# Output transposes in 64-row halves, and a plain product for the last 128 slots of the last expert

## The chip, the core and the metric

The kernel runs on one core of a Trainium2 chip. The core has five engines with instruction streams of their own: TensorE (PE; its weight loads are listed as PEld), VectorE (DVE), ScalarE (ACT), GpSimd (POOL) and SyncE (SP), and DMA queues that SP, ACT and POOL fill. They wait for each other through semaphores. The metric is the device time in microseconds (us) of one execution; lower is better. The profile is of one execution on its own.

## The reference

The first half is attention with a threshold, for 8 batches of 8 heads with 576 rows of 64: scores below the row's maximum less `tau` are dropped. Its output, as rows of 512, goes through one of eight experts, chosen by a hash of the token:

```python
scores = scale * np.matmul(q, k.transpose(0, 1, 3, 2))
thresh = np.max(scores, axis=-1, keepdims=True) - tau
scores = np.where(scores >= thresh, scores, -1000000000.0)
attn = np.exp(scores - np.max(scores, axis=-1, keepdims=True))
attn = attn / (np.sum(attn, axis=-1, keepdims=True) + 1e-09)
x = np.matmul(attn, v)                            # then (B,H,S,D) -> (B*S, H*D)
expert_idx = token_ids * np.int64(2654435761) % np.int64(E)
for e in range(E):                                # E = 8, N = 4608, D = 512, F = 1024
    mask = expert_idx == e
    h = np.maximum(x[mask] @ w1[e], 0.0)
    out[mask] = h @ w2[e]
```

## The kernel before

**Stages.** Attention runs over 32 pairs of heads and writes x to a scratch in DRAM. Beside it the tokens are sorted into slots: each expert has `CAP` = 608 slots, in five tiles (`kt` 0 to 4) of 128, 128, 128, 128 and 96. `stok` holds the token of every slot, and `gidx` the same as a table with a column per expert and tile, which the output scatters use (lines 744 to 750). From about 504 us on the experts run, one after the other. What doesn't fit into 608 slots is left to an overflow loop at line 989, which runs `n_ov` times, a number read from SBUF; with these inputs its body is skipped.

**An expert.** Activations lie transposed, features on partitions, slots along the free axis. Layer 1 is x times w1 with a Relu, layer 2 is h times w2. Both are done by `seven` (line 825), a Strassen-like scheme: each operand is cut into 2 by 2 blocks, seven block products take the place of eight, and sums of blocks are made on DVE. The slots are halved into `CH` = 304 columns, so a product streams 304 columns. A product of layer 2 is 8 matmuls in the source, each of which is two instructions on TensorE: 16 of 128 by 128 weights. `left` and `right` (lines 783 to 791) list the four sums of the weights and of the activations. They write one sum over one of the blocks itself (`a21` and `b12`), the other three into `w1_s`, `w2_s`, `x_s`, `h_s`. Each product lands in a PSUM tile of two banks (`bank2`, four of them in turn); ACT copies the first one to `p1`, and DVE adds the rest through `u2`, `u3`, `u4` into the outputs: h in layer 1, `oT` in layer 2.

**Output.** `oT` holds an expert's result transposed, 512 features as four blocks (`co`) of 128 partitions, by 608 slots. `put_out` (line 876) turns the named tiles back with TensorE transposes of 128 by 128 (line 882), copies each turned tile to an `o_sb` buffer (three in turn) and scatters its rows to `out` with an indirect DMA from POOL (line 894). Two tiles share one PSUM tile, one bank each.

**Order.** The order on each engine is the order in the source (`manual_schedule`), with side work hung between the seven products: `side1` and `side2` are called after each step. Expert e - 1's outputs go out in layer 1 of expert e, tiles (0, 1) after step 0, (2, 3) after step 1, (4) after step 2. The last expert has no successor: its tiles (0, 1) go out after step 4 of its layer 2, ahead of the seventh product, and (2, 3) and (4) when that is done (lines 977 and 978). SP loads the weights of later experts and moves turned x; POOL gathers x and scatters outputs.

**The same transposes elsewhere.** In the attention stage `turn` (line 266) and `early_xT` (line 554) turn 64 rows at a time: the two halves of the partitions, one after the other, into two different banks.

Of the kernel before, what the change touches and what calls it, by code (L numbers as in the profile page):

```python
# [9 lines left out]
FP32 = mybir.dt.float32  # L10
# [10 lines left out]
def kernel(  # L21
# [35 lines left out]
    KT, NB = 5, 19  # L57
    CAP = 32 * NB
# [69 lines left out]
    with tc.tile_pool(name="a_q", bufs=1) as a_q, \  # L128
# [496 lines left out]
        with tc.manual_schedule():  # L625
# [119 lines left out]
            for h in range(4):  # L745
                rows, n = slice(32 * h, 32 * h + 32), (NB - h + 3) // 4
                nc.vector.tensor_copy(gidx[rows, :, 0:n], stok[rows, :, h::4])
            for g in range(4):
                rows, n = slice(32 * g, 32 * g + 32), min(KT, NB - KT * g)
                nc.vector.tensor_copy(gidx_x[rows, 1:, 0:n], stok[rows, 1:, KT * g:KT * g + n])  # L750
# [8 lines left out]
    with tc.tile_pool(name="m_x", bufs=1) as m_x, \  # L759
# [4 lines left out]
        xT_bufs = [xT_0, m_x.tile([P, CO, CAP], FP32, name="xT_1")]  # L764
        xq = m_x.tile([P, DIN // 32, 32 * KT], FP32, name="xq")
        oT = m_x.tile([P, CO, CAP], FP32, name="oT")
        mark = m_x.tile([P, 1], FP32, name="mark")
        w1_s = m_s.tile([P, 3, C2, F2], FP32, name="w1_s")
        x_s = m_s.tile([P, 3, C2, CH], FP32, name="x_s")
        w2_s = m_s.tile([P, 3, FH, D2], FP32, name="w2_s")  # L770
        h_s = m_s.tile([P, 3, FH, CH], FP32, name="h_s")
        p1, u2, u3, u4 = (m_s.tile([P, 2, CH], FP32, name=n) for n in ("p1", "u2", "u3", "u4"))

        def bank2():
            return ps_m[0].tile([P, 2, 512], FP32, name="bank2")

        def sub(out, in0, in1):
            return lambda: nc.vector.tensor_tensor(out=out, in0=in0, in1=in1, op=ALU.subtract)

        def add(out, in0, in1):  # L780
            return lambda: nc.vector.tensor_tensor(out=out, in0=in0, in1=in1, op=ALU.add)  # L781

        def left(a11, a12, a21, a22, s):

            s2, s3, s4 = s
            return [sub(s3, a11, a21), add(a21, a21, a22), sub(s2, a21, a11), sub(s4, a12, s2)]

        def right(b11, b12, b21, b22, t):

            t2, t3, t4 = t  # L790
            return [sub(t3, b22, b12), sub(b12, b12, b11), sub(t2, b22, b12), sub(t4, b21, t2)]
# [4 lines left out]
        def w2_blocks(w):  # L796
            return [w[:, FH * j:FH * j + FH, D2 * i:D2 * i + D2] for i in range(2) for j in range(2)]
# [1 line left out]
        def x_blocks(x):  # L799
            return [x[:, C2 * j:C2 * j + C2, CH * k:CH * k + CH] for j in range(2) for k in range(2)]  # L800

        def h_blocks(c0, c1):
            return [h_0[:, FH * j + c0:FH * j + c1, CH * k:CH * k + CH]
                    for j in range(2) for k in range(2)]

        def triple(t, c0, c1):
            return [t[:, i, c0:c1] for i in range(3)]

        def sums_w1(e):
            return left(*w1_blocks(w_tiles[e, 1]), triple(w1_s, 0, C2))  # L810

        def sums_w2(e):
            return left(*w2_blocks(w_tiles[e, 2]), triple(w2_s, 0, FH))

        def sums_x(e):
            return right(*x_blocks(xT_bufs[e % 2]), triple(x_s, 0, C2))

        def sums_h(c0, c1):
            return right(*h_blocks(c0, c1), triple(h_s, c0, c1))

        def run(work, n=1):
            for _ in range(min(n, len(work))):
                work.pop(0)()

        def seven(a, a_s, b, b_s, m0, outs, relu, after):

            (a11, a12, s1, a22), (s2, s3, s4) = a, a_s
            (b11, t1, b21, b22), (t2, t3, t4) = b, b_s
            c11, c12, c21, c22 = outs
            n_k = a11.shape[1]  # L830

            def product(x, y):
                ps = bank2()
                for i in range(2):
                    c0 = m0 + P * i
                    for c in range(n_k):
                        nc.tensor.matmul(ps[:, i, 0:CH], lhsT=x[:, c, c0:c0 + P], rhs=y[:, c],  # L837
                                         start=c == 0, stop=c == n_k - 1)
                return ps[:, :, 0:CH]

            def out(c, ps, u, step):
                add(c, ps, u)()
                if relu:
                    nc.scalar.activation(c, c, AF.Relu)  # L844
                after(step)

            nc.scalar.copy(p1[:], product(a11, b11))  # L847
            out(c11, product(a12, b21), p1[:], 0)
            add(u2[:], product(s2, t2), p1[:])()
            after(1)  # L850
            add(u3[:], product(s3, t3), u2[:])()
            after(2)
            out(c21, product(a22, t4), u3[:], 3)
            k5 = product(s1, t1)
            add(u4[:], k5, u2[:])()
            out(c22, k5, u3[:], 4)
            out(c12, product(s4, b22), u4[:], 5)

        def layer1(e, side):

# [6 lines left out]

        def layer2(e, side):

            w = w_tiles.pop((e, 2))  # L870
            outs = [oT[:, C2 * i:C2 * i + C2, CH * k:CH * k + CH]
                    for i in range(2) for k in range(2)]
            seven(w2_blocks(w), triple(w2_s, 0, FH), h_blocks(0, FH), triple(h_s, 0, FH), 0, outs,
                  False, side)

        def put_out(e, kts):

            tr = bank2()
            for i, kt in enumerate(kts):
                rows = TROWS[kt]  # L880
                for co in range(CO):
                    nc.tensor.transpose(tr[0:rows, i, P * co:P * co + P],  # L882
                                        oT[:, co, FIRST[kt]:FIRST[kt] + rows], ident[:])
            for i, kt in enumerate(kts):
                rows = TROWS[kt]
                o_sb = m_o.tile([P, DIN], FP32, name="o_sb")
                if e == E - 1 and kt % 2:
                    nc.vector.tensor_copy(o_sb[0:rows], tr[0:rows, i])
                else:
                    nc.scalar.copy(o_sb[0:rows], tr[0:rows, i])  # L890
                put_rows(o_sb[0:rows], gidx[0:rows, e, kt:kt + 1])

        def put_rows(o_sb, idx):
            inst = nc.gpsimd.indirect_dma_start(  # L894
                out=out[:, :], out_offset=bass.IndirectOffsetOnAxis(ap=idx, axis=0),
                in_=o_sb, in_offset=None, bounds_check=N - 1, oob_is_err=False)
# [28 lines left out]
        with tc.tile_pool(name="ps_x", bufs=1, space=PSUM) as ps_x, tc.manual_schedule():  # L925
            run(sums_w2(0), 4)
            fill(18)
            late_h(lambda fo: (ps_sc.tile([P, 2, 512], FP32, name="sc") if fo in (2, 4) else
                               ps_x.tile([P, 2, 512], FP32, name="xT_ps")))
            fetch(1)  # L930
            run(sums_h(0, FH), 4)
        sc_stack.close()
        ps_m = [ctx.enter_context(tc.tile_pool(name="ps_m", bufs=4, space=PSUM))]

        with tc.manual_schedule():
            for e in range(E):
                more = e + 1 < E
                turns = turn_x(e + 1) if more else []

                if e > 0:  # L940
                    w2_work, h_work = sums_w2(e), sums_h(0, 2)
# [16 lines left out]
                    run(sums_h(2, FH), 4)  # L958
                if e + 2 < E:
                    load_w1(e + 2)  # L960
                x_work = (sums_w1(e + 1) + sums_x(e + 1)) if more else []

                def side2(step):
                    if step == 0:
                        run(turns, len(turns))
                        if e + 2 < E:
                            fetch(e + 2)
                    else:
                        run(x_work, 2)
                    if not more and step == 4:  # L970
                        put_out(e, (0, 1))

                layer2(e, side2)
                run(x_work, len(x_work))
                if e + 2 < E:
                    load_w2(e + 2)
            put_out(E - 1, (2, 3))
            put_out(E - 1, (4,))

        def relu_layer(w_sb, x_sb):  # L980
            for fo in range(FO):
# [71 lines left out]
```

## Time and profile before

| what | value |
| --- | --- |
| median of 3 runs | 956.54 us (956.51 to 958.95) |
| profiled execution, its own time | 963.93 us |
| its span, first to last instruction | 962.3 us |
| TensorE clock granted, mean | 0.997 |
| PE busy | 941.3 us, 98% |
| DVE, ACT, POOL busy | 738.2, 479.6, 302.4 us |
| all transposes of line 882 | 160 |
| all output scatters of line 894 | 40 |

An engine's busy time is read as a share of the span. PE at 98% means that its own work and what keeps it waiting set nearly all of the time. A row of the timeline names the start and length in us, the engine, the line, the operation, output<-input, the shape and how many instructions were merged. Matmuls overlap in the pipe, so that the length of one (0.419 us for 304 columns) is more than the distance to the next; the distances are what adds up. The rows of POOL's DMA_INDIRECT are the time to write the descriptors; the data moves afterwards.

### The profile page before, as it was taken

The numbers are of one execution on the slowest core, as the hardware profiler recorded it, in microseconds if no ns is written. First come the engines' busy times: TensorE is split into PE (matmuls) and PEld (weight loads), VectorE is DVE, ScalarE is ACT, GpSimd is POOL, SyncE is SP. The second block draws the span as 40 slices with busy tenths as digits, with TensorE's granted clock in tenths as the row PEclk, the third lists the DMA queues.
The fourth block names the chain that finished last, engine by engine and source line by source line (L and its number), as shares of the span: only waits on it lengthen the run. The fifth ranks groups of instructions, "written<-read, shape, count | busy, mean of one in ns | idle before, by whom it ended". The sixth has DMA issues, their size and how long they took to land.

```text
span 962.3 us, 20672 instructions
## 1 busy us (share of the span) xinstructions
PE 941.3 (98%) x7595; PEld 646.8 (67%) x7595; DVE 738.2 (77%) x1631; ACT 479.6 (50%) x777; POOL 302.4 (31%) x413
## 2 busy tenths in 40 slices
PE   7999999999999999999999999999999999999995
PEld 4666666666566666656667777777777777777774
DVE  8999999999999999999446666756657556675541
ACT  6988898888888888888220211202112031120310
POOL 4233233346666633564043300303013030100202
PEclk9999999999999999999999999999999999999998
DMA  7445445544546857631016444344433445211101
GB/s 181 97 121 146 116 111 141 135 111 110 125 99 177 212 154 199 157 93 32 26 45 208 161 106 159 95 141 161 129 127 103 140 152 158 108 53 25 50 1 50
DMA packets 113397, 113.41 MB, mean 118 GB/s; under 512 B 27476, under 2 KB 87896, under 8 KB 113296
## 3 DMA queue, kind: packets, MB, share of 16 engines
q1 hardware_dynamic: 105168, 92.95, 35.7%
q0 software_dynamic: 7696, 18.91, 6.4%
q8 instruction: 62, 1.02, 0.4%
q14 instruction: 39, 0.32, 0.1%
q10 hardware_dynamic: 432, 0.21, 0.1%
HBM read 81.99 MB, written 21.85 MB: 108 GB/s over the span
## 4 chain that ended last, share of the span: by engine, by line
PE 79%; issue 16%; DVE 1%; ACT 1%; POOL 1%; DMA 1%; SPq 0%; POOLq 0%; DVEq 0%; ACTq 0%
PE bank L837 29%; PE av L297 18%; PE sc L219 15%; PE tr L266 11%; PE sc L578 3%; PE av L266 2%; PE bank L882 1%; POOL out_dram L894 1%; ACT w L244 1%; DVE w L255 1%; PE xT_ps L595 0%; PE sc L595 0%; DVE ns L230 0%; ACT wT_b L287 0%; DMA out_dram<-o_sb,gidx 0%
## 5 line engine op out<-in xcount | busy, mean ns | idle before, releaser
L244 ACT ACTIVATE w<-ns,nmx 128x576 f32<-128x576 f32 x288 | 220.4, 777 | 27.0 <-DVE ns L230 26.8
L255 DVE SCALAR_TENSOR_TENSOR w<-ns,thr,w 128x576 f32<-128x576 f32 x288 | 225.4, 815 | 0.0
L230 DVE TENSOR_SCALAR_CACHE_REDUCE ns<-sc 128x576 f32<-128x576 f32 x288 | 205.6, 746 | 7.5 <-PE sc L219 6.7
L219 PE MATMUL sc<-k_sb,q 64*128 64x288 f32 (+1 forms) x1280 | 177.2, 421 | 1.2 <-DVE drop L641 0.5
L266 PEld LDWEIGHTS tr<-ident,w 64*128 64x128 f32 x2624 | 106.1, 139 | 95.5 <-ACT wT_b L287 32.2
L237 POOL TENSOR_SCALAR thr<-nmx,drop 128x2 f32<-128x2 f32 (+1 forms) x160 | 103.8, 649 | 189.3 <-DVE ns L230 176.7
L266 PE MATMUL tr<-ident,w 64*128 64x64 f32 x2624 | 139.6, 231 | 6.6 <-ACT wT_b L287 2.6
L894 POOL DMA_INDIRECT out_dram<-o_sb,gidx x40 | 47.9, 1198 | 302.0 <-ACT o_sb L890 294.7
L847 ACT COPY p<-bank 128x608 f32<-128x608 f32 x22 | 14.6, 665 | 205.1 <-PE bank L837 205.0
L219 PEld LDWEIGHTS sc<-k_sb,q 64*128 64x128 f32 (+1 forms) x1280 | 92.9, 177 | 21.8 <-DVE ns L230 8.1
L837 PE MATMUL bank<-h,w_sb 128*128 128x304 f32 x384 | 101.0, 419 | 0.9 <-DVE h L600 0.9
L297 PE MATMUL av<-wT_a,v 128*64 128x320 f32 (+1 forms) x704 | 100.4, 418 | 0.0
L844 ACT ACTIVATE h<-h 128x608 f32<-128x608 f32 x56 | 39.8, 710 | 114.6 <-DVE h L781 111.9
L287 ACT COPY wT_a<-tr 128x512 f32<-128x512 f32 (+1 forms) x128 | 81.7, 639 | 20.5 <-PE tr L266 20.2
L837 PEld LDWEIGHTS bank<-h,w_sb 128*128 128x128 f32 x384 | 72.9, 190 | 26.5 <-DVE h L600 1.4
L837 PE MATMUL bank<-xT,w_sb 128*128 128x304 f32 x336 | 90.5, 419 | 0.0
L287 ACT COPY wT_b<-tr 128x512 f32<-128x512 f32 (+1 forms) x128 | 81.3, 635 | 16.0 <-PE tr L266 8.9
L297 PE MATMUL av<-wT_b,v 128*64 128x256 f32 x640 | 83.2, 389 | 0.0
L837 PEld LDWEIGHTS bank<-xT,w_sb 128*128 128x128 f32 x336 | 63.8, 190 | 22.1
L837 PE MATMUL bank<-h_s,w_s 128*128 128x304 f32 x256 | 66.8, 419 | 0.0
L297 PEld LDWEIGHTS av<-wT_a,v 128*64 128x64 f32 x704 | 43.8, 136 | 28.5
L781 DVE TENSOR_TENSOR u<-bank,u 128x608 f32<-128x608 f32 x44 | 34.3, 780 | 35.1 <-PE bank L837 35.0
(139 smaller groups left out, 1141.0 us busy)
## 6 DMA issues: line engine op xcount, KB each, us to landing
w_sb<-in_moe_w_dram SPq DMA_DIRECT2D x16, 2048.0 KB
q<-in_q_dram SPq DMA_DIRECT2D x62, 288.0 KB
v<-in_v_dram SPq DMA_DIRECT2D x32, 256.0 KB
x_scratch<-xm SPq DMA_DIRECT2D x32, 256.0 KB
xT<-xq SPq DMA_DIRECT2D x84, 80.0 KB
k_sb<-in_k_dram SPq DMA_DIRECT2D x31, 144.0 KB
k_sb<-in_k_dram SPq DMA_DIRECT2D x32, 112.0 KB
x_scratch<-xg SPq DMA_DIRECT2D x9, 256.0 KB
```

What stands on the lines that cost most here:

```text
L219: nc.tensor.matmul(sc[out_rows, i, 0:S2], lhsT=q_sb[rows, h, q0:q1], rhs=k_sb[rows, h], start=True, stop=True)
L230: nc.vector.tensor_scalar(out=ns[:].rearrange("p (i s) -> p i s", i=2), in0=sc[:, :, 0:S2], scalar1=-1.0, scalar2=None, op0=ALU.mult, op1= ...
L237: nc.gpsimd.tensor_scalar(out=thr[:, 0:j + 1], in0=stats[n][0][:, 0:j + 1], scalar1=drop[:], scalar2=None, op0=ALU.add)
L244: nc.scalar.activation(w, nss[n, j][:], AF.Exp, bias=stats[n][0][:, j:j + 1], scale=-1.0)
L255: nc.vector.scalar_tensor_tensor(out=w, in0=nss.pop((n, j))[:], scalar=stats[n][1][:, j:j + 1], in1=w, op0=ALU.is_le, op1=ALU.mult, accum_ ...
L266: nc.tensor.transpose(dst[:, r, 64 * c:64 * c + 64], src[rows, c0:c0 + P], ident[rows, rows])
L287: nc.scalar.copy(dst, tr[:, :, 0:64 * n_c].rearrange("p r (c q) -> p r c q", c=n_c))
L297: nc.tensor.matmul(av[64 * j:64 * j + 64, g, c0:c1], lhsT=v_sb[:, c, 64 * j:64 * j + 64], rhs=wT[g][:, i, c0:c1], start=(c == 0), stop=stop)
L781: return lambda: nc.vector.tensor_tensor(out=out, in0=in0, in1=in1, op=ALU.add)
L837: nc.tensor.matmul(ps[:, i, 0:CH], lhsT=x[:, c, c0:c0 + P], rhs=y[:, c], start=c == 0, stop=c == n_k - 1)
L844: nc.scalar.activation(c, c, AF.Relu)
L894: inst = nc.gpsimd.indirect_dma_start(out=out[:, :], out_offset=bass.IndirectOffsetOnAxis(ap=idx, axis=0), in_=o_sb, in_offset=None, bound ...
```

## The change

Three things change.

1. `put_out` turns 64 rows at a time, for all experts. For each block it issues two transposes, of partitions 0 to 63 and of 64 to 127, into bank 0 and bank 1 of the PSUM tile. Their 64 columns for four blocks fill half a bank, so that two slot tiles still share a PSUM tile. The copies gather the halves back into order through a rearranged access pattern.
2. In the last expert, `seven` covers the first 480 slots only: halves of `CHL` = 240 columns. The sums of h are made over 240 columns too. The sum that `left` wrote over `a21` goes into a spare buffer of the `w1_sb` pool, so that w2 stays as loaded.
3. The last 128 slots of the last expert are computed by `last_tile`: h times w2 as a plain product with slots as rows, which needs no transposes; 384 output columns, then 128. Halfway through the first part it calls `middle`, which puts out tiles (1, 2) and (3), the latter of 96 rows; tile 0 alone goes out after step 4. Its result goes through a new buffer, `o_end`, and one scatter. `gidx` gets the tokens of the last 128 slots in the last expert's column 4, with four more small copies.

```diff
@@ tables of output rows
             for h in range(4):
                 rows, n = slice(32 * h, 32 * h + 32), (NB - h + 3) // 4
                 nc.vector.tensor_copy(gidx[rows, :, 0:n], stok[rows, :, h::4])
+                nc.vector.tensor_copy(gidx[rows, E - 1, KT - 1:KT],
+                                      stok[rows, E - 1, NB - 4 + h:NB - 3 + h])
@@ sums
-        def left(a11, a12, a21, a22, s):
+        def left(a11, a12, a21, a22, s, s1=None):
+            s1 = a21 if s1 is None else s1
             s2, s3, s4 = s
-            return [sub(s3, a11, a21), add(a21, a21, a22), sub(s2, a21, a11), sub(s4, a12, s2)]
+            return [sub(s3, a11, a21), add(s1, a21, a22), sub(s2, s1, a11), sub(s4, a12, s2)]
+        def half2(e):
+            return CH if e < E - 1 else CHL
         def sums_w2(e):
-            return left(*w2_blocks(w_tiles[e, 2]), triple(w2_s, 0, FH))
+            s1 = None
+            if e == E - 1:
+                spare = w_pool.tile([P, CO, F], FP32, name="w1_sb")
+                s1 = w_tiles["s1"] = spare[:, :, 0:D2]
+            return left(*w2_blocks(w_tiles[e, 2]), triple(w2_s, 0, FH), s1)
@@ seven
-                        nc.tensor.matmul(ps[:, i, 0:CH], lhsT=x[:, c, c0:c0 + P], rhs=y[:, c],
+                        nc.tensor.matmul(ps[:, i, 0:width], lhsT=x[:, c, c0:c0 + P], rhs=y[:, c],
@@ the last 128 slots
+        def last_tile(middle):
+            w, o_sb, idx = w_tiles[E - 1, 2], o_end, gidx[:, E - 1, KT - 1:KT]
+            for c0, c1 in ((0, DIN - P), (DIN - P, DIN)):
+                ps = bank2()
+                for fo in range(FO):
+                    nc.tensor.matmul(ps[:, 0, 0:c1 - c0], lhsT=h_0[:, fo, CAP - P:CAP],
+                                     rhs=w[:, fo, c0:c1], start=fo == 0, stop=fo == FO - 1)
+                    if (c0, fo) == (0, FH - 1):
+                        middle()
+                nc.scalar.copy(o_sb[:, c0:c1], ps[:, 0, 0:c1 - c0])
+            put_rows(o_sb[:], idx)
@@ put_out
-                rows = TROWS[kt]
+                rows = TROWS[kt] if e < E - 1 or kt < KT - 2 else CAP - P - FIRST[kt]
                 for co in range(CO):
-                    nc.tensor.transpose(tr[0:rows, i, P * co:P * co + P],
-                                        oT[:, co, FIRST[kt]:FIRST[kt] + rows], ident[:])
+                    for r in range(2):
+                        half, c0 = slice(64 * r, 64 * r + 64), D2 * i + 64 * co
+                        nc.tensor.transpose(tr[0:rows, r, c0:c0 + 64],
+                                            oT[half, co, FIRST[kt]:FIRST[kt] + rows],
+                                            ident[half, half])
...
+                dst = o_sb[0:rows].rearrange("p (c r q) -> p r c q", c=CO, r=2)
+                src = tr[0:rows, :, D2 * i:D2 * i + D2].rearrange("p r (c q) -> p r c q", c=CO)
                 if e == E - 1 and kt % 2:
-                    nc.vector.tensor_copy(o_sb[0:rows], tr[0:rows, i])
+                    nc.vector.tensor_copy(dst, src)
                 else:
-                    nc.scalar.copy(o_sb[0:rows], tr[0:rows, i])
+                    nc.scalar.copy(dst, src)
@@ the end of the experts
-                        put_out(e, (0, 1))
+                        put_out(e, (0,))
...
-            put_out(E - 1, (2, 3))
-            put_out(E - 1, (4,))
+            def middle():
+                put_out(E - 1, (1, 2))
+                put_out(E - 1, (3,))
+            last_tile(middle)
```

More of the change, by code (lines that the diff above doesn't have):

```diff
@@ L766 @@
         oT = m_x.tile([P, CO, CAP], FP32, name="oT")
+        o_end = m_x.tile([P, DIN], FP32, name="o_end")
         mark = m_x.tile([P, 1], FP32, name="mark")
@@ L771 @@
         h_s = m_s.tile([P, 3, FH, CH], FP32, name="h_s")
-        p1, u2, u3, u4 = (m_s.tile([P, 2, CH], FP32, name=n) for n in ("p1", "u2", "u3", "u4"))
+        halves = [m_s.tile([P, 2, CH], FP32, name=n) for n in ("p1", "u2", "u3", "u4")]
+        CHL = (CAP - P) // 2
         def bank2():
@@ L800, in x_blocks, with h_blocks, triple @@
             return [x[:, C2 * j:C2 * j + C2, CH * k:CH * k + CH] for j in range(2) for k in range(2)]
-        def h_blocks(c0, c1):
-            return [h_0[:, FH * j + c0:FH * j + c1, CH * k:CH * k + CH]
+        def h_blocks(c0, c1, half):
+            return [h_0[:, FH * j + c0:FH * j + c1, half * k:half * k + half]
                     for j in range(2) for k in range(2)]
-        def triple(t, c0, c1):
-            return [t[:, i, c0:c1] for i in range(3)]
+        def triple(t, c0, c1, width=None):
+            return [t[:, i, c0:c1, 0:width] for i in range(3)]
+        def half2(e):
+            return CH if e < E - 1 else CHL
         def sums_w1(e):
@@ L812, in sums_w2, with sums_h @@
         def sums_w2(e):
-            return left(*w2_blocks(w_tiles[e, 2]), triple(w2_s, 0, FH))
+            s1 = None
[3 more added lines that the diff above has]
+            return left(*w2_blocks(w_tiles[e, 2]), triple(w2_s, 0, FH), s1)
         def sums_x(e):
             return right(*x_blocks(xT_bufs[e % 2]), triple(x_s, 0, C2))
-        def sums_h(c0, c1):
-            return right(*h_blocks(c0, c1), triple(h_s, c0, c1))
+        def sums_h(e, c0, c1):
+            return right(*h_blocks(c0, c1, half2(e)), triple(h_s, c0, c1, half2(e)))
         def run(work, n=1):
@@ L829, in seven @@
             c11, c12, c21, c22 = outs
-            n_k = a11.shape[1]
+            n_k, width = a11.shape[1], b11.shape[2]
+            p1, u2, u3, u4 = (t[:, :, 0:width] for t in halves)
             def product(x, y):
@@ L836, in product @@
                     for c in range(n_k):
-                        nc.tensor.matmul(ps[:, i, 0:CH], lhsT=x[:, c, c0:c0 + P], rhs=y[:, c],
+                        nc.tensor.matmul(ps[:, i, 0:width], lhsT=x[:, c, c0:c0 + P], rhs=y[:, c],
                                          start=c == 0, stop=c == n_k - 1)
-                return ps[:, :, 0:CH]
+                return ps[:, :, 0:width]
             def out(c, ps, u, step):
@@ L845, in out @@
                 after(step)
-            nc.scalar.copy(p1[:], product(a11, b11))
-            out(c11, product(a12, b21), p1[:], 0)
-            add(u2[:], product(s2, t2), p1[:])()
+            nc.scalar.copy(p1, product(a11, b11))
+            out(c11, product(a12, b21), p1, 0)
+            add(u2, product(s2, t2), p1)()
             after(1)
-            add(u3[:], product(s3, t3), u2[:])()
+            add(u3, product(s3, t3), u2)()
             after(2)
-            out(c21, product(a22, t4), u3[:], 3)
+            out(c21, product(a22, t4), u3, 3)
             k5 = product(s1, t1)
-            add(u4[:], k5, u2[:])()
-            out(c22, k5, u3[:], 4)
-            out(c12, product(s4, b22), u4[:], 5)
+            add(u4, k5, u2)()
+            out(c22, k5, u3, 4)
+            out(c12, product(s4, b22), u4, 5)
         def layer1(e, side):
@@ L868, in layer2 @@
         def layer2(e, side):
-            w = w_tiles.pop((e, 2))
-            outs = [oT[:, C2 * i:C2 * i + C2, CH * k:CH * k + CH]
+            w, half = w_tiles[e, 2], half2(e)
+            outs = [oT[:, C2 * i:C2 * i + C2, half * k:half * k + half]
                     for i in range(2) for k in range(2)]
-            seven(w2_blocks(w), triple(w2_s, 0, FH), h_blocks(0, FH), triple(h_s, 0, FH), 0, outs,
-                  False, side)
+            a = w2_blocks(w)
+            if e == E - 1:
+                a[2] = w_tiles["s1"]
+            seven(a, triple(w2_s, 0, FH), h_blocks(0, FH, half),
+                  triple(h_s, 0, FH, half), 0, outs, False, side)
+        def last_tile(middle):
[9 more added lines that the diff above has]
+            put_rows(o_sb[:], idx)
         def put_out(e, kts):
@@ L879, in put_out @@
             for i, kt in enumerate(kts):
-                rows = TROWS[kt]
+                rows = TROWS[kt] if e < E - 1 or kt < KT - 2 else CAP - P - FIRST[kt]
                 for co in range(CO):
-                    nc.tensor.transpose(tr[0:rows, i, P * co:P * co + P],
-                                        oT[:, co, FIRST[kt]:FIRST[kt] + rows], ident[:])
+                    for r in range(2):
[3 more added lines that the diff above has]
+                                            ident[half, half])
             for i, kt in enumerate(kts):
-                rows = TROWS[kt]
+                rows = TROWS[kt] if e < E - 1 or kt < KT - 2 else CAP - P - FIRST[kt]
                 o_sb = m_o.tile([P, DIN], FP32, name="o_sb")
+                dst = o_sb[0:rows].rearrange("p (c r q) -> p r c q", c=CO, r=2)
+                src = tr[0:rows, :, D2 * i:D2 * i + D2].rearrange("p r (c q) -> p r c q", c=CO)
                 if e == E - 1 and kt % 2:
-                    nc.vector.tensor_copy(o_sb[0:rows], tr[0:rows, i])
+                    nc.vector.tensor_copy(dst, src)
                 else:
-                    nc.scalar.copy(o_sb[0:rows], tr[0:rows, i])
+                    nc.scalar.copy(dst, src)
                 put_rows(o_sb[0:rows], gidx[0:rows, e, kt:kt + 1])
@@ L930 @@
             fetch(1)
-            run(sums_h(0, FH), 4)
+            run(sums_h(0, 0, FH), 4)
         sc_stack.close()
@@ L940 @@
                 if e > 0:
-                    w2_work, h_work = sums_w2(e), sums_h(0, 2)
+                    w2_work, h_work = sums_w2(e), sums_h(e, 0, 2)
                     def side1(g, step):
@@ L957 @@
                     layer1(e, side1)
-                    run(sums_h(2, FH), 4)
+                    run(sums_h(e, 2, FH), 4)
                 if e + 2 < E:
```

## The prediction

> **What bounds the kernel now.** I read the page first: the engines' shares, then the clock.
>
> ```profile
> PE 941.3 (98%) x7595; PEld 646.8 (67%) x7595; DVE 738.2 (77%) x1631; ACT 479.6 (50%) x777; POOL 302.4 (31%) x413
> ...
> PEclk9999999999999999999999999999999999999998
> ```
>
> TensorE is busy for 98% of the span at full clock, so almost everything it is given or spared moves the end, except behind its last matmul. The list of waits says the same: from 503 us on TensorE waits 0.9 us twice, once when the experts begin and once at the end. So two places matter: the transposes between layer-1 products, and the tail.
>
> The timeline of PE shows one expert's `put_out` among the products (start, duration, engine, line, count):
>
> ```profile
> 535.70 1.19 PE L837 MATMUL bank<-xT,w_sb 128*128 128x304 f32 x4
> 536.72 1.04 PE L882 MATMUL bank<-ident,oT 128*128 128x128 f32 x8
> 537.59 2.21 PE L837 MATMUL bank<-x_s,w_s 128*128 128x304 f32 x8
> 539.64 1.04 PE L882 MATMUL bank<-ident,oT 128*128 128x128 f32 x8
> 540.51 2.21 PE L837 MATMUL bank<-x_s,w_s 128*128 128x304 f32 x8
> 542.56 0.60 PE L882 MATMUL bank<-ident,oT 128*96 128x128 f32 x4
> 543.00 0.68 PE L837 MATMUL bank<-x_s,w_sb 128*128 128x304 f32 x2
> ```
>
> Start to start, 8 transposes take 0.87, 4 take 0.44 (0.109 each); 8 products of 304 columns take 2.05 (0.256 each). A matmul of the source is two here. No gap at the borders. The new form, 64 rows in, 128 by 64 out, in pairs, is what line 266 does in the attention stage. Where it stands between products of 304 columns:
>
> ```profile
> 473.29 1.29 PE L578 MATMUL sc<-xT,w_sb 128*128 128x304 f32 x4
> 474.51 0.52 PE L266 MATMUL av<-ident,oT 64*128 64x64 f32 x10
> 474.97 5.38 PE L578 MATMUL sc<-xT,w_sb 128*128 128x304 f32 x20
> ```
>
> The first row's four should take 1.02 to the next start, but take 1.22. The single starts say why: the last product to the first pair is 0.350 instead of 0.256; first to second pair 0.111, then 0.062 a pair, the two halves 0.004 apart; last half to the product behind 0.154 instead of about 0.06; that product to the next 0.360 instead of 0.256. The burst before the last tile of `early_xT` repeats these numbers.
>
> The tail:
>
> ```profile
> 950.18 0.79 DVE L781 TENSOR_TENSOR oT<-bank,u 128x608 f32<-128x608 f32 x1 [2.79 <-PE bank L837]
> 951.03 1.53 PE L882 MATMUL bank<-ident,oT 128*128 128x128 f32 x12 [0.88 <-DVE oT L781]
> 952.16 1.07 ACT L890 COPY o_sb<-bank 128x512 f32<-128x512 f32 x2 [5.49 <-PE bank L882]
> 952.77 0.69 DVE L888 COPY o_sb<-bank 128x512 f32<-128x512 f32 x1 [1.80 <-ACT o_sb L890]
> 953.02 0.98 POOL L894 DMA_INDIRECT out_dram<-o_sb,gidx  x1 [3.80 <-ACT o_sb L890]
> 954.30 0.98 POOL L894 DMA_INDIRECT out_dram<-o_sb,gidx  x1 [0.30 <-issue]
> 955.58 0.93 POOL L894 DMA_INDIRECT out_dram<-o_sb,gidx  x1 [0.30 <-DMA out_dram<-o_sb,gidx]
> ```
>
> Product, add, transposes, copy, then three scatters at 1.28 each: POOL's queue sets the end. Behind the third, the closing instructions:
>
> ```profile
> L1049 POOLq DRAIN  x3: 46/103/2118, 959.4 to 962.0; - x3
> ```
>
> The row gives the count, least, median and greatest ns, first and last start. From the third scatter's start to the first DRAIN 3.79 (landing, then the loop's exit waits), the DRAIN 2.12, 0.83 more to 962.32: 6.74 in all.
>
> **What the Trainium skill says.** "TensorEngine Tiling (Array Packing)", Key Properties: changing the tiling mode drains TensorE, while tiles work independently. The trace agrees: 0.094 + 0.050 + 0.092 + 0.104 = 0.34 a round trip, and halves 0.004 apart. Instruction Overhead there: a 60-cycle floor under small matmuls; the trace's 0.062 a pair against 0.109 for 128 columns fits. "DMA: Bandwidth & Descriptors", Anatomy of one DMA: about 2 us fixed on the gpsimd path, mostly completion; the 3.79 holds it. "Runtime: NRT & Kernel Launch", Instruction fetch mechanics: a taken branch can stall on a fetch. No row separates this from the DRAIN's 2.12; that is the open number here.
>
> **The change, part by part.** Times are against the profiled span of 962.32 (execution 963.93); the median 956.54 is 5.8 below the span, and I take the same difference off it.
>
> 1. Transposes of experts 0 to 6. A burst of 8 pairs, last product before to second product behind: 0.350 + 0.111 + 6 x 0.062 + 0.004 + 0.154 + 0.360 = 1.351. Now: 0.256 + 7 x 0.109 + 0.109 + 0.259 = 1.387. Gain 0.036. A burst of 4 pairs: 1.103 against 0.951, loss 0.152. Per expert two of one and one of the other: loss 0.08; seven experts: **+0.57**. Halving the streamed columns is eaten by the mode changes. The copies read both banks; line 287 does that for 512 elements in 0.56 to 0.6, line 890 takes 0.585, and ACT idles most of this stage: nothing. If a copy grew by 0.1, the products still cover it (a bank returns after four tiles).
>
> 2. Four copies into `gidx`, one column each, on DVE at 476.4. The row of line 747 has 0.196 apiece: +0.8 to +0.9. Late next is the copy of `early_h` at 479.25, which would end near 480.9. TensorE needs its bank at 481.2 (12 products of 0.256 from 474.97, twice, plus the mode change): hidden, with 0.3 to spare, as are the two copies behind it. Uncovered it would cost at most 0.5.
>
> 3. Last expert, layer 2, from its first matmul at X = 920.45. The pitch at 240 columns is 0.256 less 64 x 0.00084 = 0.2025 (slope from 304 and 128 columns). Six products of 16: 19.44 (was 24.56). Tile 0's burst of 4 pairs: 0.094 + 0.239 + 0.154 + 0.104 = 0.59 (was 0.88). Product 7: 3.24 (was 4.09). So the plain product starts at T = X + 23.28; product 7 ended at X + 29.53 before. DVE's sums shrink too and stay hidden behind the first two products. The separate `s1` goes into a weight buffer whose reader, expert 6's layer 1, is long done. Tile 0's scatter, alone at step 4, has run by T - 1.3 and landed by T + 0.4, before tile 3 takes its buffer; SP has nothing in its queue here, and POOL nothing else.
>
> 4. Plain product. Eight matmuls of 384 columns (0.323): 2.58. The add of the last product ends at about T + 0.95, so the transposes don't wait for it. 12 pairs with both mode changes: 1.09. The first 16 are readable at T + 3.45; the DVE copy, 0.69, ends at T + 4.14; POOL starts 0.28 behind (as 953.02 behind 952.74): scatters at T + 4.42, 5.70, 6.98. TensorE's rest: 2.58 + 16 x 0.109 = 1.75, last write T + 8.2, copy of 128 columns about 0.27: `o_end` is full at T + 8.5.
>
> 5. Where the last scatter stands. In the built program's instruction order on POOL, the scatter of `o_end` isn't with the other three: it stands behind the exit of the overflow loop, after its waits. So the exit waits follow the scatter at T + 6.98: 6.98 + 3.79 = T + 10.77, later than `o_end` (8.5) by over 2. TensorE's last 4.5 us are thus hidden. Then the scatter: 0.19 to start and 0.98 to run (rows of line 894), T + 11.94; DRAIN 2.12, close 0.83: T + 14.9 = X + 38.2, with part 1 X + 38.75. Before: X + 41.87. **Gain 3.1**: the third scatter starts 4.87 earlier, less 0.57, less 1.17 for the fourth behind the exit.
>
> Nothing waits for that last scatter's data but the end of the program.
>
> The unknown is how DRAIN and the fourth scatter combine. Lower end: the 2.12 was a fetch or fixed work that runs beside the scatter: 1.0 less, gain 4.1. Upper end: DRAIN first waits until the scatter has landed (in the trace the wait on the last scatter ends 2.72 after its start) and then takes its 2.12: 1.7 more, gain 1.4. I take the plain sum in between, since before no scatter was open when it began and it lasted 2.12 all the same.
>
> **Rivals.** (a) DRAIN waits for the landing: gain 1.4, about 955.1. For it: scatters are POOL's own descriptors. Against: nothing names such a wait. (b) DRAIN overlaps the scatter: gain 4.1, about 952.4. (c) Slower: between products the halves run one behind the other. Then 20 pairs per expert cost 0.06 more each, 1.2 x 7 = 8.4, and the last expert's 12 pairs ahead of its three scatters 0.75: 3.1 - 9.15, about 962.6. It decides from 0.44 more per expert. Against it: line 266 between products at 474.51, ten in 0.45. (d) The mode changes cost nothing here: 21 x 0.34 = 7.1 more gain and 0.5 in the last expert, about 946. Against it the same row. (e) The change does not do what it says, the fourth scatter being merely in line with the rest: it would start at T + 8.8, end X + 23.28 + 0.57 + 8.8 + 6.74 = X + 39.4, gain 2.5; the instruction order excludes it.
>
> **How the numbers follow.** About 0.3%, 2.9 us, is what a measurement here tells from no change; that line is 953.67. Forecast 0.56, with gains of 2.6 to 3.6, about two thirds of it beyond the line; (a) and cases between it and the forecast 0.21; (b) 0.13; (d) 0.04; (c) and an uncovered wait of similar size 0.06. Faster: 0.37 + 0.13 + 0.04 = 0.54; slower 0.06; same 0.40. The time is that of the forecast, 956.54 - 3.1 = 953.4. The range holds the forecast, (a) and (b) with 0.3 to 0.4 of spread: 952.0 to 955.5; (c) and (d) are left out.
>
> **What will show it.** Right: in experts 0 to 6 bursts of 16 taking 0.64 from their start to the next product's and bursts of 8 taking 0.39, with 0.1 more in the product on each side; product 7 ending near 944.3; three scatters near 948.7, 950 and 951.3; the fourth near 955.3, long after the last copy; DRAIN near 2.1; span near 959.2. Wrong in part 1 if the mode changes differ by 0.1 (0.1 x 21 = 2.1 us); in part 5 if DRAIN differs, or if the branch into the new block behind the loop stalls (then up to 2 us more). Wrong in part 2 if TensorE pauses near 481 to 488.

## The result, and the profile after

The changed kernel has a median of 955.16 us in 20 runs (954.26 to 956.47). The kernel before, run 20 times beside it, has 957.0 us (956.42 to 959.58). The ratio of the means is 0.9976, with a 95% interval of 0.997 to 0.9983: 2.3 us faster, between 1.6 and 2.9 (the medians lie 1.84 apart). The forecast was 953.4 and a gain of 3.1. The time lies in the forecast's range, 0.3 us from its upper end. The interval doesn't reach to no change, so the gain is real, but it is smaller than forecast and under the 2.9 us that the prediction took for the least that can be told from no change.

The two profiled executions differ by far more, 962.32 against 953.96 us of span. Most of that isn't the change. Expert 0's first layer-2 matmul starts at 503.87 before and at 497.58 after; that is 6.29 of the 8.36. Here it is, with expert 7's first, in the timeline of before:

```profile
503.87 0.52 PE L837 MATMUL bank<-h,w_sb 128*128 128x304 f32 x1 [0.88 <-DVE h L600]
920.45 0.42 PE L837 MATMUL bank<-h,w_sb 128*128 128x304 f32 x1
```

and of after:

```profile
497.58 0.52 PE L850 MATMUL bank<-h,w_sb 128*128 128x304 f32 x1 [0.88 <-DVE h L600]
914.60 0.37 PE L850 MATMUL bank<-h,w_sb 128*128 128x240 f32 x1
```

Seven of the experiments below have the same attention stage as the changed kernel, and that matmul starts between 502.1 and 505.9 in them; in the one that has the attention stage of before, it starts at 503.1. Also, the profiled execution of before (963.93) is 7 us above its kernel's median. In the 20 runs it started near 496.9 before and 497.1 after; these are estimates, the medians less the profile's length from that matmul on and less the 1.6 to 1.7 by which a profiled execution's time exceeds its span. So I read from that matmul to the end of the span: 458.46 before, 456.38 after, a gain of **2.07**, which lies inside the interval.

The first lines of the page after, as they were shown for before:

```profile
PE 940.5 (99%) x7779; PEld 646.1 (68%) x7779; DVE 735.8 (77%) x1635; ACT 479.4 (50%) x778; POOL 305.3 (32%) x413
...
PEclk9999999999999999999999999999999999999999
```

184 more TensorE instructions than before (312 halves in place of 160 transposes, and 32 of the plain product), and 0.8 us less busy: TensorE still fills the stage. The timeline of PE in the kernel after, at one expert's `put_out` (start, duration, engine, line, count):

```profile
526.34 4.26 PE L850 MATMUL bank<-xT,w_sb 128*128 128x304 f32 x16
530.52 0.72 PE L913 MATMUL bank<-ident,oT 64*128 64x64 f32 x16
531.17 2.31 PE L850 MATMUL bank<-x_s,w_s 128*128 128x304 f32 x8
533.42 0.72 PE L913 MATMUL bank<-ident,oT 64*128 64x64 f32 x16
534.07 2.31 PE L850 MATMUL bank<-x_s,w_s 128*128 128x304 f32 x8
536.31 0.43 PE L913 MATMUL bank<-ident,oT 64*96 64x64 f32 x8
```

Sixteen halves take 0.65 from their start to the next product's; the eight full transposes took 0.87. But the eight products behind them take 2.25 to the next start instead of 2.05, because the first and the last of them stand next to a mode change. Sum: 2.90 now, 2.92 before.

The tail, timeline of the kernel after:

```profile
937.88 2.74 PE L898 MATMUL bank<-w_sb,h 128*128 128x384 f32 x8
...
940.55 0.94 PE L913 MATMUL bank<-ident,oT 64*128 64x64 f32 x24
941.31 1.28 DVE L922 COPY o_sb<-bank 128x512 f32<-128x512 f32 x2 [2.58 <-PE bank L913]
...
942.28 0.98 POOL L928 DMA_INDIRECT out_dram<-o_sb,gidx  x1 [5.79 <-DVE o_sb L922]
943.56 0.98 POOL L928 DMA_INDIRECT out_dram<-o_sb,gidx  x1 [0.30 <-issue]
...
944.85 0.93 POOL L928 DMA_INDIRECT out_dram<-o_sb,gidx  x1 [0.30 <-issue]
946.09 0.27 ACT L902 COPY o_end<-bank 128x128 f32<-128x128 f32 x1 [1.31 <-PE bank L898]
949.33 0.99 POOL L928 DMA_INDIRECT out_dram<-o_end,gidx  x1 [3.55 <-issue]
```

With T = 937.88, the start of the plain product: three scatters at T + 4.40, 5.69 and 6.97; `o_end` full at T + 8.5; and its scatter only at T + 11.45, 3.0 us after its data was there. Then the closing instructions of the kernel after (count, least, median and greatest ns, first and last start):

```profile
L1088 POOLq DRAIN  x3: 46/109/4007, 949.1 to 953.7; - x3
```

The long DRAIN takes 4.007, where before it took 2.118. Its record opens at 949.10, before the scatter's own at 949.33, and ends at 953.11, which is 3.78 us after the scatter's start.

### The profile page after: what moved, and what is told of

It reads as the page before. It is cut to its first block, busy times and chain, and to the rows that moved or that the text cites. A ratio compares the mean times of both kernels' runs of the same rounds, so it can differ in the third digit from the quotient of the medians.

```text
span 954.0 us, 21044 instructions
## 1 busy us (share of the span) xinstructions
PE 940.5 (99%) x7779; PEld 646.1 (68%) x7779; DVE 735.8 (77%) x1635; ACT 479.4 (50%) x778; POOL 305.3 (32%) x413
## 3 DMA queue, kind: packets, MB, share of 16 engines
q8 instruction: 63, 1.03, 0.5%
## 5 line engine op out<-in xcount | busy, mean ns | idle before, releaser
L860 ACT COPY p<-bank 128x608 f32<-128x608 f32 (+1 forms) x22 | 14.5, 661 | 204.3 <-PE bank L850 204.2
L850 PE MATMUL bank<-h,w_sb 128*128 128x304 f32 (+1 forms) x384 | 98.4, 413 | 0.9 <-DVE h L600 0.9
L850 PE MATMUL bank<-h_s,w_s 128*128 128x304 f32 (+1 forms) x256 | 65.1, 412 | 0.0
L850 PE MATMUL bank<-x_s,w_s 128*128 128x304 f32 x224 | 62.2, 426 | 0.0
```

What stands on the lines that cost most here:

```text
L850: nc.tensor.matmul(ps[:, i, 0:width], lhsT=x[:, c, c0:c0 + P], rhs=y[:, c], start=c == 0, stop=c == n_k - 1)
L860: nc.scalar.copy(p1, product(a11, b11))
```

## The experiments

Each was read by the same two lengths: the *stage*, from expert 0's first layer-2 matmul to expert 7's (416.586 before, 417.024 after), and *T to the end* of the span (16.08 after). The kernel before, which took 957.0 us beside the changed kernel, took 967.59 us beside `e1_full_turns`, `e3_inline`, `e4_five_bursts` and `e6_drain_big` (one run, chip 14) and 963.9 us beside the others (median of 11, chip 7). All but the last experiment are single runs, whose whole times carry the attention stage's variation, so the two lengths decide. These repeat well: the five kernels with three bursts of halves per expert have a stage of 417.016 to 417.024, and in four kernels with the same tail T to the end is 16.08 to 16.09.

**Part 1 undone.** Experts 0 to 6 turned by full transposes again; the last expert as changed.

```diff
                 for co in range(CO):
+                    if e < E - 1:
+                        nc.tensor.transpose(tr[0:rows, i, P * co:P * co + P],
+                                            oT[:, co, FIRST[kt]:FIRST[kt] + rows], ident[:])
+                        continue
                     for r in range(2):
...
-                if e == E - 1 and kt % 2:
+                if e < E - 1:
+                    nc.scalar.copy(o_sb[0:rows], tr[0:rows, i])
+                elif kt % 2:
```

> The changed kernel with the outputs of experts 0 to 6 turned in 128x128 again; the last expert stays as changed. Theory M (each change of tiling mode costs about 0.34 us a round trip, a pair of halves 0.062): the stage from the first layer-2 product of expert 0 to that of expert 7 takes 416.6 us as before, instead of the changed kernel's 417.0; the tail from the plain product on stays at 16.1 us. Rival (the 0.4 come from the copies or from waits of the products on them): the stage stays at 417.0 or moves by something else than 0.06 an expert.

Measured: stage 416.586, to the nanosecond that of before; T to the end 16.09; 961.45 us in all. The halves in experts 0 to 6 cost 0.44 and give nothing. From expert 0's matmul to the end this kernel takes 455.95, 0.43 less than the changed one.

**Part 1 alone**, in the kernel before: the transposes and copies of the diff's `put_out`, nothing else.

```diff
-                    nc.tensor.transpose(tr[0:rows, i, P * co:P * co + P],
-                                        oT[:, co, FIRST[kt]:FIRST[kt] + rows], ident[:])
+                    for r in range(2):
+                        half, c0 = slice(64 * r, 64 * r + 64), D2 * i + 64 * co
+                        nc.tensor.transpose(tr[0:rows, r, c0:c0 + 64],
+                                            oT[half, co, FIRST[kt]:FIRST[kt] + rows],
+                                            ident[half, half])
...
```

> The kernel before with part 1 alone: transposes in halves, the last expert otherwise as before. Theory M: the stage from expert 0's to expert 7's first layer-2 product 417.0 us instead of 416.6; from there to the end about 41.5 instead of 41.9, because the last transposes, which follow an idle gap, are shorter by 0.3. Rival (halving the columns pays between products too): stage below 416.6.

Measured: stage 417.020; from expert 7's first layer-2 matmul to the end 41.501, where before it is 41.869; 963.23 us in all. The last expert wins 0.37, its long burst ahead of the last scatters being shorter; the other seven lose 0.43. The sum, 458.52 against 458.46, is nothing. So the gain comes from the last expert's new layout, the second and third point of the change: 2.51 (458.46 less 455.95) with experts 0 to 6 turned in full, and 2.07 with them in halves. No run takes the shorter products, the plain product and the new order of the scatters apart.

**More bursts.** Five bursts of one tile per expert in place of three.

```diff
-                            if step == 0:
-                                put_out(e - 1, (0, 1))
-                            elif step == 1:
-                                put_out(e - 1, (2, 3))
-                            elif step == 2:
-                                put_out(e - 1, (4,))
+                            if step < KT:
+                                put_out(e - 1, (step,))
```

> The changed kernel with each expert's outputs (0 to 6) in five bursts of one tile, after steps 0 to 4, instead of three: the same transposes, two more round trips of the tiling mode per expert. Theory M: 2 x 0.334 more per expert, 4.7 us in all, the stage 417.0 -> 421.7. Rival (the cost sits in the transposes or copies, not in the mode changes): the stage stays within 0.5 of 417.0.

Measured: stage 421.781, 4.757 longer than after: 0.340 for each of the 14 bursts added. T to the end 16.09; 966.31 us in all. The same 20 pairs are in it, so the price hangs on the bursts and not on the transposes in them. Full transposes pay nothing at the borders of their bursts (0.256 and 0.259 from start to start before), so that the price is that of going to halves and back: the change of mode.

**One burst.** All 20 pairs of an expert behind step 2, into three PSUM tiles, and five `o_sb` buffers instead of three.

```diff
-          tc.tile_pool(name="m_o", bufs=3) as m_o, \
+          tc.tile_pool(name="m_o", bufs=5) as m_o, \
...
+        def put_all(e):
+            groups = ((0, 1), (2, 3), (4,))
+            trs = [bank2() for _ in groups]
+            for tr, kts in zip(trs, groups):
+                for i, kt in enumerate(kts):
...
+                            nc.tensor.transpose(tr[0:rows, r, c0:c0 + 64],
...
+            for tr, kts in zip(trs, groups):
+                for i, kt in enumerate(kts):
...
+                    nc.scalar.copy(dst, src)
+                    put_rows(o_sb[0:rows], gidx[0:rows, e, kt:kt + 1])
...
-                            if step == 0:
-                                put_out(e - 1, (0, 1))
-                            elif step == 1:
-                                put_out(e - 1, (2, 3))
-                            elif step == 2:
-                                put_out(e - 1, (4,))
+                            if step == 2:
+                                put_all(e - 1)
```

> The changed kernel with all five output tiles of experts 0 to 6 turned in one burst of 20 pairs after step 2 (three PSUM tiles in a row, five buffers o_sb instead of three), two round trips of the tiling mode fewer per expert. Theory M: 0.70 less per expert, 4.9 in all, stage 417.0 -> 412.1. Rival (three PSUM tiles in a row, or five copies in a row on ACT, hold up the products): the stage gains less than 3 or gets longer, and TensorE shows waits for DVE or ACT in layer 1.

Measured: stage 412.267, 4.757 shorter than after (0.340 per burst saved, the same size, which leaves nothing for the two added buffers) and 4.32 shorter than before; T to the end 16.09; 955.43 us in all, beside 963.9. The timeline of PE in this kernel:

```profile
534.94 4.26 PE L850 MATMUL bank<-x_s,w_s 128*128 128x304 f32 x16
539.13 1.45 PE L937 MATMUL bank<-ident,oT 64*128 64x64 f32 x40
540.51 2.31 PE L850 MATMUL bank<-x_s,w_sb 128*128 128x304 f32 x8
542.66 2.21 PE L850 MATMUL bank<-xT,w_sb 128*128 128x304 f32 x8
```

40 halves take 1.38 us to the next product's start, where the 20 full transposes of before took 0.87 + 0.87 + 0.44 = 2.18. The 16 matmuls ahead take 4.19 instead of 4.10, the 8 behind 2.15 instead of 2.05, and then it is 2.05 again: one mode change there and back, paid once. The halves pay when a burst is long enough to carry its mode change. This is what "TensorEngine Tiling (Array Packing)" in the Trainium skill, Key Properties, leads to: changing the mode drains TensorE. The 0.340 is this kernel's figure for it.

**The last scatter in line.** The read of `n_ov` moved to behind `last_tile`, inside the hand-ordered stretch, which keeps `o_end`'s scatter with the other three, ahead of the loop.

```diff
             last_tile(middle)
+            n_ov = nc.values_load(ov_i[0:1, NOV:NOV + 1], min_val=0, max_val=NOV)
...
-        n_ov = nc.values_load(ov_i[0:1, NOV:NOV + 1], min_val=0, max_val=NOV)
         with tc.For_i(0, n_ov, 1) as it:
```

> The changed kernel with the scatter of the last 128 slots ahead of the overflow loop (the load of the loop's count stands behind it in the source). T is the start of the plain product. Theory D (the closing DRAIN of POOL waits for the scatter that is still open): the scatter starts at T + 8.8, the DRAIN is 2.1 us again, the end at T + 15.5 instead of T + 16.1. Rival F (the longer DRAIN is a stall at the branch or a fixed cost that another program layout has too): the DRAIN stays near 4.0 and the end is near T + 17.4.

Measured: the fourth scatter at T + 8.754, and the DRAIN of this kernel:

```profile
L1088 POOLq DRAIN  x3: 46/103/2118, 957.9 to 960.5; - x3
```

That is before's row again, 2.118 and 103: once the loop's exit has waited for the scatter, the DRAIN is short. But the end was T + 16.27, 0.19 later than in the changed kernel, against an expected 15.5. The missing 0.77 lies between the scatter's start and the DRAIN: 4.56 instead of the 3.79 of before. Most of it is a late landing: the scatter's last packet ended 2.99 after its start, where the last scatter of before took 2.35. The DMA queues of this kernel between 953.2 and 956.4 (packets, MB, share of 16 engines; q0 has this scatter and the end of the one ahead) show what else was moving:

```profile
q0 software_dynamic: 127, 0.36, 32.0%
q8 instruction: 1, 0.02, 2.6%
```

The one packet of q8, 16384 bytes of instructions, runs from 953.91 to 955.26. Of the scatter's 80 packets 75 have ended by 955.65, which is 2.35 after its start. The other five, one sixteenth of them, run one behind the other from 955.28, 0.02 after the instruction packet's end, to 956.29. This reads as one of the 16 DMA engines being held by the instruction packet; the trace doesn't name the engines. Beside the last scatter of before and of after runs no instruction packet. Without the 0.64 us the end would be near T + 15.6 (estimate), close to the 15.5 expected. Whether the packet falls there in every execution one run can't say. 962.57 us in all. In this run both orders end within 0.2 us of each other: in line, the exit waits for the scatter; behind the exit, the DRAIN does.

**Does the DRAIN wait for transfers?** One more DMA of POOL behind the loop, 2.49 MB from `h_0` to a scratch that nobody reads.

```diff
+    spill = nc.dram_tensor("spill_scratch", (P, FO, CAP), FP32, kind="Internal").ap()
...
             put_rows(o_sb[:], idx[:, 0:1])
+        nc.gpsimd.dma_start(out=spill, in_=h_0[:])
```

> The changed kernel with a further POOL transfer behind the loop: h (2.49 MB) to a scratch in DRAM that nobody reads. Theory D: the DRAIN waits for its landing, 12 to 16 us at 150 to 200 GB/s, so DRAIN and span are over 8 us longer. Rival F (DRAIN waits for the descriptors at most): DRAIN longer by the issue alone, 1 to 2 us.

The POOL rows of its timeline and its closing DRAIN:

```profile
955.00 0.98 POOL L929 DMA_INDIRECT out_dram<-o_end,gidx  x1 [3.56 <-issue]
955.97 0.61 POOL L1059 DMA_DIRECT2D spill_scratch<-h  x1
```

```profile
L1090 POOLq DRAIN  x3: 46/109/9607, 955.2 to 965.4; - x3
```

The DRAIN lasts 9.607 instead of 4.007 and T to the end is 22.15 instead of 16.08. The transfer's packets run from 957.31 to 963.35, and the DRAIN ends at 964.85, 1.5 behind the last; in the changed kernel the DRAIN ends 1.42 behind the scatter's last packet, in `e1_full_turns` 1.43. So the DRAIN waits until POOL's open transfers have landed, and needs some 1.4 more. The transfer took 6.0 us, some 410 GB/s, where 150 to 200 GB/s were expected; hence the forecast of over 8 us, where 6.07 were added. 967.48 us in all.

**Is TensorE's end hidden?** `middle` after the second matmul of the plain product instead of the fourth: the same work, the turned tiles 1.29 earlier, TensorE's last matmul where it was.

```diff
-                    if (c0, fo) == (0, FH - 1):
+                    if (c0, fo) == (0, 1):
                         middle()
```

> The changed kernel with the outputs of tiles 1 to 3 put out after the second matmul of the plain product instead of the fourth. TensorE's work is the same. Theory P (POOL's three scatters and the exit waits behind them set the end, TensorE's last 4.5 us are hidden): the three scatters, the exit and the end come 1.29 earlier, the end at T + 14.8 instead of T + 16.1. Rival (TensorE's last matmul sets the end): the end stays at T + 16.1.

Measured: T to the end 14.771, 1.31 less; scatters at T + 3.11, 4.40, 5.69 and T + 10.16; TensorE's last matmul starts at T + 7.90 as before the edit. 962.72 us in all. The three scatters and what stands behind them set the end; the plain product's second half has slack, as point 5 said.

**A version from both**: one burst per expert, and the early `middle`; against the changed kernel, with `put_all` as above:

```diff
-          tc.tile_pool(name="m_o", bufs=3) as m_o, \
+          tc.tile_pool(name="m_o", bufs=5) as m_o, \
...
-                    if (c0, fo) == (0, FH - 1):
+                    if (c0, fo) == (0, 1):
...
+                            if step == 2:
+                                put_all(e - 1)
```

> Both together: one burst of 20 pairs per expert, and tiles 1 to 3 of the last expert put out after the second matmul. If theories M and P hold, 4.9 + 1.3 = 6.2 us below the changed kernel, so about 2.3 + 6.2 = 8.5 us or 0.9% below the kernel before, a ratio near 0.991. If the products wait for the burst, no better than 0.996.

Measured in six runs: 955.04 us median (954.62 to 958.09) beside 963.9 (962.61 to 967.34, eleven runs) for the kernel before, ratio 0.9912 (0.9893 to 0.9931), or 8.5 us. Stage 412.262, T to the end 14.815. Both single effects add: from expert 0's matmul to the end 450.35, 6.03 less than the changed kernel and 8.11 less than before.

| kernel | stage | T to the end | expert 0 to the end | long DRAIN |
| --- | --- | --- | --- | --- |
| before | 416.586 | no plain product | 458.46 | 2.118 |
| after | 417.024 | 16.08 | 456.38 | 4.007 |
| part 1 undone | 416.586 | 16.09 | 455.95 | 4.004 |
| part 1 alone | 417.020 | no plain product | 458.52 | 2.118 |
| five bursts | 421.781 | 16.09 | 461.14 | 3.994 |
| one burst | 412.267 | 16.09 | 451.63 | 4.004 |
| scatter in line | 417.016 | 16.27 | 456.56 | 2.118 |
| transfer behind the loop | 417.018 | 22.15 | 462.44 | 9.607 |
| early `middle` | 417.021 | 14.77 | 455.07 | 3.993 |
| one burst, early `middle` | 412.262 | 14.82 | 450.35 | 4.013 |

## Why the prediction was right or wrong

**Part 1, a loss in experts 0 to 6: right, a little oversized.** Forecast +0.57 (its own 0.08 per expert is 0.56), measured +0.44 (undone: 416.586 again). The burst of 8 pairs was 1.362 where the attention stage's numbers gave 1.351. The burst of 4 pairs was 1.069 instead of 1.103, because its tile has 96 rows: the first pair took 0.098, the others 0.056, the exit 0.145. With five bursts, 4 pairs of 128 rows take 1.105. The prediction read the 0.062 of a pair as fitting a fixed floor under small matmuls; that 96 rows take 0.056 at the same 64 streamed columns speaks for a part that depends on the tile's rows. Rivals (c), halves one behind the other, and (d), free mode changes, are out: pairs take 0.062, and each burst pays 0.340.

**Part 2, hidden copies: right.** TensorE waits for nothing between the copies and the experts, and from the attention stage's last transpose to expert 0's first layer-2 matmul it takes 29.046 us, where before it took 29.051. The one wait of 0.9 at the start of the experts is there as before. The copies lengthened their stretch on DVE by 0.6, not by 0.8 to 0.9.

**Part 3: right.** T lies 23.276 behind X (forecast 23.28); 240 columns take 0.2025 as interpolated.

**Part 4: right.** Scatters at T + 4.40, 5.69, 6.97 (4.42, 5.70, 6.98); `o_end` full at T + 8.5.

**Part 5, the last scatter behind the loop's exit: the place was right, what the DRAIN does there was wrong, and the sum was 1.2 us too small.** The place was as said: the exit came at T + 10.69 (10.77), and the scatter after it, long after the last copy. Two terms were off. First, from the exit to the scatter 0.76 passed instead of 0.19. The exit is followed by a short instruction of POOL's queue that belongs to the scatter. Ahead of a scatter in line, from that instruction to the scatter's start is 0.23 (not 0.19), as the chain of waits of before (start, us, what) shows ahead of the first of its last three scatters:

```profile
952.78 0.03 POOLq L894
952.81 0.05 issue
952.86 0.02 POOLq L894
952.88 0.14 issue
953.02 3.50 DMA out_dram<-o_sb,gidx
```

In the chain of after, 0.51 of "issue" follow it, in which POOL did nothing that the profile shows, and the scatter's record starts only at 949.33:

```profile
948.56 0.03 POOLq L928
948.59 0.51 issue
949.10 1.21 POOLq L1088
```

The prediction listed a stall at a branch among what would make it wrong; a fetch after a taken branch is what the Trainium skill names in "Runtime: NRT & Kernel Launch", Instruction fetch mechanics. The trace doesn't show it in POOL's queue. The first instruction behind the branch came 0.12 after it, as it did ahead of the DRAIN of before. The next instruction behind the scatter came 0.54 after that first one; behind the scatters in the tail of before, with no branch ahead of them, it came 0.64 to 0.73 after it. So the queue was not held up, and only the scatter's own start is late. It is as late in `e6_drain_big`, where another transfer follows and not the DRAIN. No run took the branch away and left the scatter where it is, so the cause stays open. Second, "0.98 to run; DRAIN 2.12" took the scatter's writing as the only thing the DRAIN follows. It took 3.78 from the scatter's start to the DRAIN's end instead of 3.10, because the DRAIN waits for the landing. By the prediction's own sign, a DRAIN near 2.1, part 5 was wrong. The terms: -0.08 + 0.57 + 0.68 and 0.02 at the close = 1.19.

**The rivals on the tail.** (a) has the right mechanism: the transfer behind the loop lengthened the DRAIN with it. Its price was too high, as the 2.12 isn't added whole behind the landing; some 1.4 is. The forecast's step "I take the plain sum in between" chose wrongly: the 2.12 of before had said nothing on an open scatter, since there the exit had waited for all of them. (b), overlap, is out. (e), a scatter in line, is not what the change does, and the experiment that did it ended at T + 16.27, its landing late behind the instruction packet.

So the profile's gain was 3.67 - 1.16 from X on (the 1.19 of above, but for rounding) and 0.44 lost ahead of it: 2.07. The measured time of 955.16 is 1.8 above the forecast: 1.03 is this shortfall, 0.46 that the kernel before had 957.0 in these runs instead of the 956.54 it was reckoned from, and the rest, about 0.3, is within what runs scatter. The time lies in the range because the range was drawn to hold (a) as well. That it lies next to (a)'s 955.1 is chance: (a) stood for a gain of 1.4, and the shift of the kernel before made up the difference.

## What to carry to other kernels

Transposes in 64-row pairs pay only in bursts that are long enough for the mode change. Here a burst costs 0.340 us extra and a pair saves about 0.047 on a full transpose (0.109 less 0.062): 8 pairs about break even (1.362 us against 1.388), 20 in one burst gave 4.3 us over seven experts. At the end of a program, count to the landing of the last transfer of the queue that is drained, and not to its issue; to end earlier, make the earliest of the chained scatters start earlier, which cost one line here and gave 1.3 us.

## What the runs showed of the hardware that was not expected

- POOL's DRAIN at the end of the program waits for that queue's open transfers: 2.118 with none open, 4.0 with one scatter open, 9.607 with a scatter and 2.49 MB open, ending 1.42 to 1.5 after the last packet.
- Instruction packets share the DMA engines with the kernel's data, as far as the packets' times tell: in `e3_inline` five of a scatter's 80 packets came behind one of 16384 bytes, and the last landed 2.99 after the scatter's start instead of 2.35.
- From the loop's exit to the next scatter's start 0.76 to 0.78 passed, in all kernels with that order alike (T + 11.45 to 11.47 where `middle` was not moved), against 0.23 ahead of a scatter in line. The cause is open.
